# One score block in eighteen exponentiated on VectorE, with a new model of the convolution's load times

## The chip, the cores and the metric

The kernel runs on one core of one Trainium2 chip. The metric is the device time of one execution in microseconds (us). A time is the median of several executions. A profile is one execution, and its span is about 2 us shorter than the time. A core has five engines with a queue each: TensorE (PE in the profile, PEld its weight loads), VectorE (DVE), ScalarE (ACT), GpSimd (POOL) and SyncE (SP, which here issues loads). The program gives each engine one list of instructions, and before an instruction the engine waits until the semaphores that it names are reached.

## The reference

Two independent results stand side by side in the output: attention with 32 heads of 16, and a long causal convolution with gates.

```python
qkv = (x @ wqkv).reshape(B, S, 3, H, Dh).transpose(2, 0, 3, 1, 4)      # S 2048, D 512, H 32, Dh 16
scores = einsum("bhqd,bhkd->bhqk", q, k) * Dh ** -0.5
p = softmax(scores, axis=-1)
a = einsum("bhqk,bhkd->bhqd", p, v).transpose(...).reshape(B, S, D) @ wo
# ... k_shift: a 4-tap shift of B_k; kv = k_shift * B_v
y = causal_convolution(kv, ssm_k) + kv * ssm_D      # by FFT in the reference; 512 channels, 2048 taps each
b = B_q * y
out = concatenate([a, b], axis=-1)
```

The attention has 32 x 2048 x 2048 exponentials. The kernel makes them as 2048 blocks of 128 x 512.

## The kernel before

Scores lie in PSUM, three banks to a "chunk", two sets of three banks in turn. A step T of the main loop does one chunk: TensorE makes three score blocks (`emit_qk`), ScalarE exponentiates all three in one instruction of 1536 columns, TensorE multiplies earlier blocks by the values (`emit_pv`), and one piece of background work follows (`emit_bg`): convolution matmuls, projections, output products. There are 692 steps. A "group" (4 heads x 512 queries) is 64 blocks, some 21.3 steps. When it is done, `finish_group` normalises it with five VectorE instructions.

```python
    def emit_qk(T):
        # ... three matmuls of a chunk; wait for bank_free of the three banks
        h = pe.op(fn, deps)
        n = len(bl)
        h_exp[T] = act.op(lambda e: e.activation(PT[:, T % R_PT, 0:n * QB],
                                                 PS[:, banks[0]:banks[0] + n, :].rearrange("p b f -> p (b f)"),
                                                 ACT.Exp, scale=SCALE),
                          [h, h_ptfree.get(T - R_PT)])
        for bank in banks:
            bank_free[bank] = h_exp[T]
```

All background work shares one PSUM bank (`BGB`). VectorE copies each finished piece out of it ("evacuation"), and the next piece of background work waits for that copy. TensorE's next scores stand behind that piece in its list, so while it waits there it makes no scores either (one such place, with a wait of 2.26 us, is shown below).

```python
    def conv_lags(qd, n0, n1):
        # ... 4 matmuls per lag into bank BGB; after four rows-of-four:
                hh = dve.op(lambda e: e.tensor_copy(YB[:, half, :].rearrange("p (k i) -> p k i", k=4), src),
                            [h, h_yb[0]])
                bank_free[BGB] = hh
    # ...
    for T in range(NT + 3):
        if T < NT:
            emit_qk(T)
        # ...
        while pvs:
            emit_pv(pvs[:4], T)
            pvs = pvs[4:]
        emit_bg(T)
        for item in list(dve_later):      # the rest of a group's normalisation, one and two steps later
            if item[0] <= T:
                dve_later.remove(item)
                item[1]()
```

The convolution reads 512 filter matrices of 512 KB ("rows") from HBM, 12 in flight. When the program is built, a small model guesses when each four rows have landed, so that no convolution matmul is put in the queue too early:

```python
    def now(T):
        return 11.0 + 1.17 * min(T, N_EARLY) + 1.345 * max(T - N_EARLY, 0)
    # at the start: first rows expected 10.5, 16.5, 22.5 us after now(T); later 1.5 us a row
```

The softmax here doesn't subtract the row's maximum and nothing guards it: scores larger than these inputs give would overflow.

## Time and profile before

| | before |
|---|---|
| time, median of 3 runs | 989.31 us (989.12 to 989.63) |
| span of the profile | 986.4 us |
| ScalarE busy | 937.7 us (95%) |
| VectorE busy | 236.1 us (24%) |
| ScalarE idle between 150 and 950 us | 3.3 us (800 - 796.72) |

First come the busy times of the engines, their share of the span and their instructions, and the shares of the chain of waits, which is followed back from the last instruction.

```profile
PE 767.7 (78%) x12892; PEld 333.4 (34%) x12892; DVE 236.1 (24%) x386; ACT 937.7 (95%) x699; POOL 46.7 (5%) x65
...
ACT 79%; PE 11%; DVE 5%; DMA 4%; SPq 1%; issue 1%; ACTq 0%
```

Next, pieces of the same chain in order of time (start, duration, what; xN is the number of instructions merged).

```profile
119.06 21.19 DMA WR<-kz_scratch
...
144.98 134.69 ACT PT L459 x99
...
357.78 171.30 ACT PT L459 x126
```

134.69 / 99 and 171.30 / 126 both give 1.36 us for a back-to-back exponential of 1536 columns. These long runs without another engine between them mean that ScalarE is the limit. The DMA piece at 119 us is the one early place where everybody waits for the first convolution rows; ScalarE idles 7.3 us there.

The stretches view has the busy time of each engine in a window; the last three numbers are TensorE's granted clock, the DMA share and GB/s.

```profile
core 0: us, PE busy (x) PEld busy (x) DVE busy (x) ACT busy (x) POOL busy (x), PEclk, DMA share, GB/s
150.00:950.00 800.00, 611.31 (x11814) 284.26 (x11814) 139.80 (x217) 796.72 (x587) 13.61 (x18) 0.97 0.90 332
```

Two lines of the timeline show exponentials that stood alone, in the early part where TensorE is the limit (start, duration, engine, line, instruction, in brackets the idle time before and what ended it).

```profile
12.18 1.45 ACT L459 ACTIVATE PT<-PS 128x1536 bf16<-128x1536 f32 x1 [0.58 <-PE PS L452]
14.32 1.02 ACT L459 ACTIVATE PT<-PS 128x1024 bf16<-128x1024 f32 x1 [0.69 <-PE PS L452]
```

512 columns more cost 0.43 us more. That is what a block taken from ScalarE can save.

### The profile page before, as it was taken

How to read it: one execution, taken by the hardware profiler on the slowest of the kernel's cores; microseconds unless marked ns; L12 is line 12 of the kernel's file. 1: busy time of each engine (PE TensorE's matmuls, PEld its weight loads, DVE VectorE, ACT ScalarE, POOL GpSimd, SP SyncE). 2: the span in 40 equal slices, each digit the busy share in tenths (PEclk: the TensorE clock that was granted, in tenths of full speed). 3: DMA queues.
4: the chain of work that ended last, by engine and by line, in shares of the span. 5: the costliest groups of instructions: out<-in, count | busy, mean ns of one | idle time of the engine just before them, and what ended most of it. 6: DMA issues, size and time to landing. Idle time of an engine off the chain costs nothing.

```text
span 986.4 us, 27802 instructions
## 1 busy us (share of the span) xinstructions
PE 767.7 (78%) x12892; PEld 333.4 (34%) x12892; DVE 236.1 (24%) x386; ACT 937.7 (95%) x699; POOL 46.7 (5%) x65
## 2 busy tenths in 40 slices
PE   8998867878787787777777787777777787777787
PEld 3322123333333333333333333333333333333312
DVE  4778611211121210121211021212011212111111
ACT  5887869999999999999999999999999999999996
POOL 2121400000000100000001000000000000000000
PEclk9999779999999989999999999999999999999957
DMA  9441499998989999999899999998999999798300
GB/s 315 170 149 65 135 320 344 327 366 320 356 308 353 342 363 349 355 334 357 330 367 323 366 341 349 342 358 329 359 349 348 345 341 340 290 352 344 142 22 22
DMA packets 88566, 295.56 MB, mean 300 GB/s; under 512 B 11269, under 2 KB 19458, under 8 KB 88066
## 3 DMA queue, kind: packets, MB, share of 16 engines
q1 hardware_dynamic: 82114, 280.13, 76.8%
q0 software_dynamic: 3936, 12.58, 4.0%
q8 instruction: 102, 1.67, 0.7%
q10 hardware_dynamic: 2400, 1.05, 0.4%
q14 instruction: 14, 0.11, 0.0%
HBM read 287.31 MB, written 6.42 MB: 298 GB/s over the span
## 4 chain that ended last, share of the span: by engine, by line
ACT 79%; PE 11%; DVE 5%; DMA 4%; SPq 1%; issue 1%; ACTq 0%
ACT PT L459 78%; DMA WR<-kz_scratch 4%; PE PS L452 2%; PE PS L289 2%; PE PS L282 2%; PE PS L485 1%; PE PS L552 1%; PE PS L600 1%; DVE VAF L317 1%; SPq L151 1%; DVE WR L352 1%; DVE WR L356 1%; DVE KTo L311 1%; PE PS L275 1%; PE PS L393 1%
## 5 line engine op out<-in xcount | busy, mean ns | idle before, releaser
L459 ACT ACTIVATE PT<-PS 128x1536 bf16<-128x1536 f32 (+1 forms) x692 | 932.5, 1799 | 31.6 <-PE PS L452 31.5
L452 PE MATMUL PS<-QT,KTo 32*128 32x512 bf16 x2048 | 284.0, 404 | 188.1 <-ACT PT L459 181.5
L600 PE MATMUL PS<-WR,KV 128*15 128x128 bf16 (+15 forms) x8192 | 298.3, 226 | 16.7 <-DMA WR<-kz_scratch 11.1
L485 PE MATMUL PS<-PT,VAF 128*32 128x512 bf16 x2048 | 289.6, 409 | 0.9 <-DVE VAF L317 0.5
L600 PEld LDWEIGHTS PS<-WR,KV 128*13 128x13 bf16 (+15 forms) x8192 | 191.4, 107 | 40.7 <-issue 27.4
L452 PEld LDWEIGHTS PS<-QT,KTo 32*128 32x128 bf16 x2048 | 67.9, 92 | 367.1 <-ACT PT L459 332.5
L485 PEld LDWEIGHTS PS<-PT,VAF 128*32 128x32 bf16 x2048 | 69.2, 94 | 170.3 <-issue 162.5
L616 DVE CAST YB<-PS 128x512 bf16<-128x512 f32 x32 | 22.1, 691 | 372.5 <-PE PS L600 313.7
L505 DVE COPY OF<-PS 128x512 f32<-128x512 f32 x31 | 21.6, 696 | 217.6 <-PE PS L485 193.9
L275 PE MATMUL PS<-xT,WQP 128*128 128x512 bf16 x128 | 38.9, 397 | 1.2 <-ACT xT L261 0.3
L552 PE MATMUL PS<-WKV,OTN 128*128 128x512 bf16 x128 | 35.9, 398 | 1.3 <-DVE YB L616 1.1
L303 DVE CAST QT<-PS 128x512 bf16<-128x512 f32 x32 | 22.0, 689 | 50.6 <-PE PS L275 50.6
L151 POOL DMA_DIRECT2D out_dram<-OUTA x12 | 6.6, 551 | 405.3 <-DVE OUTA L560 378.9
L514 DVE STREAM_TRANSPOSE DT<-DR 128x512 f32<-128x512 f32 x32 | 23.1, 721 | 1.1
L507 DVE STREAM_TRANSPOSE DT<-OF 128x512 f32<-128x512 f32 x31 | 22.8, 734 | 1.1
L151 POOL DMA_DIRECT2D out_dram<-QN x4 | 4.7, 1172 | 379.3 <-DVE QN L636 379.3
L520 DVE TENSOR_TENSOR OTN<-OF,DT 128x512 bf16<-128x512 f32 x31 | 22.1, 714 | 0.8
L282 PE MATMUL PS<-xT,WKV 128*128 128x512 bf16 x64 | 18.3, 413 | 3.2 <-DVE KTo L311 1.1
L289 PE MATMUL PS<-WKV,xT 128*128 128x512 bf16 x64 | 16.6, 382 | 1.5 <-DVE xT L263 0.2
L352 DVE TENSOR_TENSOR WR<-WR 128x1024 bf16<-128x1024 bf16 x24 | 16.3, 683 | 0.0
L552 PEld LDWEIGHTS PS<-WKV,OTN 128*128 128x128 bf16 x128 | 9.8, 101 | 18.8 <-issue 9.5
L151 POOL DMA_DIRECT2D WR<-in_B_k_dram x20 | 13.9, 701 | 40.3 <-DVE KV L361 30.3
(53 smaller groups left out, 175.5 us busy)
## 6 DMA issues: line engine op xcount, KB each, us to landing
WR<-kz_scratch SPq DMA_DIRECT2D x512, 512.0 KB, 7.6
WR<-in_B_k_dram POOLq DMA_DIRECT2D x16, 256.0 KB, 4.9
kz_scratch<-WR SPq DMA_DIRECT2D x1, 2176.0 KB, 8.9
KV<-in_A_x_dram SPq DMA_DIRECT2D x4, 512.0 KB, 6.6
QN<-in_B_q_dram POOLq DMA_DIRECT2D x4, 512.0 KB, 11.3
out_dram<-QN POOLq DMA_DIRECT2D x4, 512.0 KB, 7.9
WR<-in_B_v_dram SPq DMA_DIRECT2D x6, 256.0 KB, 3.2
QT<-in_B_k_dram POOLq DMA_DIRECT2D x6, 256.0 KB, 4.3
```

The lines of the kernel that those rows point to most:

```text
L151: f(outp, inp).then_inc(dsem.sem, 16)
L275: return e.matmul(PS[:, bank, :], lhsT=WQP[:, dc, g, :], rhs=xT[:, dc, qb * 512:(qb + 1) * 512], start=(dc == 0), stop=(dc == 3))
L282: return e.matmul(PS[:, bank, :], lhsT=WK[:, dc, o * 128:(o + 1) * 128], rhs=xT[:, dc, sc * 512:(sc + 1) * 512], start=(dc == 0), stop=(dc ...
L289: return e.matmul(PS[:, bank, :], lhsT=xT[:, dc, kt * 128:(kt + 1) * 128], rhs=WV[:, dc, :], start=(dc == 0), stop=(dc == 3))
L352: st[m] = dve.op(lambda e: e.tensor_tensor(b[m], b[m], in1, ALU.mult), [h_kv[(j, 0)], h_kv[(j, 1)], h_tb[m]])
L452: ins = e.matmul(PS[:, bank, :], lhsT=KTo[32 * s:32 * s + 32, g // 2, kt * 128:(kt + 1) * 128], rhs=QT[32 * s:32 * s + 32, qb % 2, g, :], ...
L459: h_exp[T] = act.op(lambda e: e.activation(PT[:, T % R_PT, 0:n * QB], PS[:, banks[0]:banks[0] + n, :].rearrange("p b f -> p (b f)"), ACT.E ...
L485: ins = e.matmul(PS[32 * s:32 * s + 32, pvb(qb * NG + g), :], lhsT=VAF[:, kt, h * VW:h * VW + 32], rhs=PT[:, Tc % R_PT, j * QB:(j + 1) * Q ...
L507: h_t = dve.op(lambda e: e.transpose(out=DT[:, r, :], in_=src), [h_of, h_otn.get(n - 2)])
L514: st["h"] = dve.op(lambda e: e.transpose(out=DT[:, r, :].rearrange("p (b i) -> p b i", i=32), in_=rcp.broadcast_to([128, 16, 32])), [h])
L552: ins = e.matmul(PS[:, bank, :], lhsT=OTN[:, oslot(qb * NG + g), t * 128:(t + 1) * 128], rhs=WOP[:, g, :], start=(g == 0), stop=(g == NG - 1))
L600: ins = e.matmul(PS[32 * c:32 * c + NB - n, BGB, 128 * (kk % 4):128 * (kk % 4) + 128], lhsT=KV[:, n:NB, d], rhs=WR[:, d % R_W, 128 * (NB - ...
```

## The change

VectorE is idle three quarters of the time, and ScalarE is the limit. So the last block of some chunks is exponentiated on VectorE. By the rule of the change 113 chunks from step 86 on are touched, one block in each, at most four to a group (chunks 2, 7, 12 and 17 of it); that is one in 18 of the 2048 blocks; ScalarE's instruction in such a chunk has 1024 columns. VectorE scales the scores so that the integer part of the exponential's base-2 logarithm falls into the exponent field of a floating-point number, splits exponent and fraction by bit operations, and evaluates a quartic in the fraction. That gives the exponential times a constant 2 / C4. So that all blocks of a row agree, ScalarE's exponentials get the same factor: a bias of ln(2 / C4), read from a tile `EB` of one number per partition. Softmax divides the factor out again.

The model of load times is changed too: the first rows are expected later, a row is taken to need 1.3 instead of 1.5 us, and the steps are timed anew.

```diff
+    h_eb = dve.op(lambda e: e.memset(EB[:], math.log(2.0 / C4)))
+    on_dve = {}
+    for T in range(N_EARLY + 30, NT):
+        # ... n: the group, t0: its first chunk
+        if len(bl) == 3 and n == blk_group(bl[0]) and (T - t0) % 5 == 2 and T <= chunk_of[last_blk[n]][0] - 3 and 0 < kt < KT - 1:
+            on_dve[bl[-1]] = len(on_dve)
@@ emit_qk
-        n = len(bl)
+        n = len(bl) - (bl[-1] in on_dve)
-                                                 ACT.Exp, scale=SCALE),
+                                                 ACT.Exp, bias=EB[:, 0:1], scale=SCALE),
+        if n < len(bl):
+            bank_free[banks[n]] = exp_on_dve(bl[n], banks[n], h, T)
+    def exp_on_dve(b, bank, h, T):
+        h1 = dve.op(lambda e: e.tensor_scalar(EI[:, :], PS[:, bank, :], FIX, FIX_LO, ALU.mult, ALU.max), [h, h_eo[0]])
+        # split(): EM = (EI & 0x7fffff) | 0x3f800000; EI = (EI & 0x7f800000) ^ 0x40000000
+        # horner(j): EH = (src + B) * m, three times;  last(): PTD = (EH + B0) * EI as fp32, to bf16
+        dve_fill.extend([(T, split), (T + 1, lambda: horner(0)), (T + 1, lambda: horner(1)),
+                         (T + 2, lambda: horner(2)), (T + 2, last)])
+        return h1
@@ now, emit_bg
-        return 11.0 + 1.17 * min(T, N_EARLY) + 1.345 * max(T - N_EARLY, 0)
+        t1 = N_EARLY + 30
+        return 12.0 + 1.36 * min(T, t1) + 1.266 * max(T - t1, 0)
-            st["dma"] = now(T) + 3.0
+            st["dma"] = now(T) + 18.0
             for i in range(R_W // 4):
-                st["dma"] += 6.0
-                    st["dma"] = max(st["dma"], now(T) + 3.0) + 1.5
+                    st["dma"] = max(st["dma"], now(T) + 3.0) + 1.3
@@ the values' matmul of a moved block comes 5 steps after its chunk instead of 2
-        t = chunk_of[b][0] + 2
+        t = chunk_of[b][0] + (5 if b in on_dve else 2)
@@ main loop
+        for item in list(dve_fill):
+            if item[0] <= T:
+                dve_fill.remove(item)
+                item[1]()
         emit_bg(T)
```

More of the change, by code (lines that the diff above doesn't have):

```diff
@@ L1 @@
+import math
 import concourse.bass as bass
@@ L7 @@
 FP32 = mybir.dt.float32
+INT32 = mybir.dt.int32
 S = 2048
@@ L33 @@
 LAGS = 5
+C4 = 0.013534167911703966
+B0, B1, B2, B3 = 37.6797618003151, 23.053950042922654, 12.310574509367148, -0.15702561410827162
+LOG2E = 1.4426950408889634
+FIX = SCALE * LOG2E * 2.0 ** 23
+FIX_LO = -126.0 * 2.0 ** 23
 class Eng:
@@ L124, in bass_concat_heads__mha_block__ssm_conv_h3__prompt_kernel @@
     SHK = sb("SHK", [128, 4, 4])
+    PTD = sb("PTD", [128, 2, QB])
+    EI = sb("EI", [128, QB], INT32)
+    EM = sb("EM", [128, QB], INT32)
+    EH = sb("EH", [128, QB], FP32)
+    EB = sb("EB", [128, 1], FP32)
     JNK = sb("JNK", [128, 2], FP32)
@@ L432, in pvb @@
         return BGB if n == 1 else PVB
-    h_exp = {}
-    h_ptfree = {}
     chunk_of = {}
@@ L439, in bass_concat_heads__mha_block__ssm_conv_h3__prompt_kernel, with blk_group @@
             chunk_of[b] = (T, j)
+    def blk_group(i):
+        qb, g, kt, s = blk(i)
+        return qb * NG + g
+    on_dve = {}
+    for T in range(N_EARLY + 30, NT):
+        bl = chunks[T][0]
+        qb, g, kt, s = blk(bl[-1])
+        n = qb * NG + g
+        t0 = chunk_of[first[n]][0]
+        if len(bl) == 3 and n == blk_group(bl[0]) and (T - t0) % 5 == 2 and T <= chunk_of[last_blk[n]][0] - 3 and 0 < kt < KT - 1:
+            on_dve[bl[-1]] = len(on_dve)
+    h_exp = {}
+    h_blk = {}
+    h_ptfree = {}
     def emit_qk(T):
@@ L457, in emit_qk, with split, horner, last @@
         h = pe.op(fn, deps)
-        n = len(bl)
+        n = len(bl) - (bl[-1] in on_dve)
         h_exp[T] = act.op(lambda e: e.activation(PT[:, T % R_PT, 0:n * QB],
                                                  PS[:, banks[0]:banks[0] + n, :].rearrange("p b f -> p (b f)"),
-                                                 ACT.Exp, scale=SCALE),
-                          [h, h_ptfree.get(T - R_PT)])
-        for bank in banks:
-            bank_free[bank] = h_exp[T]
+                                                 ACT.Exp, bias=EB[:, 0:1], scale=SCALE),
+                          [h, h_ptfree.get(T - R_PT), h_eb])
+        for b, bank in zip(bl[:n], banks):
+            bank_free[bank] = h_blk[b] = h_exp[T]
+        if n < len(bl):
+            bank_free[banks[n]] = exp_on_dve(bl[n], banks[n], h, T)
+    h_eo = [None]
+    h_ptd = {}
+    def exp_on_dve(b, bank, h, T):
+        i = on_dve[b]
+        m = EM[:, :].bitcast(FP32)
+        st = {}
+        h1 = dve.op(lambda e: e.tensor_scalar(EI[:, :], PS[:, bank, :], FIX, FIX_LO, ALU.mult, ALU.max), [h, h_eo[0]])
+        def split():
+            st["m"] = dve.op(lambda e: e.tensor_scalar(EM[:, :], EI[:, :], 0x7fffff, 0x3f800000,
+                                                       ALU.bitwise_and, ALU.bitwise_or), [h1])
+            st["e"] = dve.op(lambda e: e.tensor_scalar(EI[:, :], EI[:, :], 0x7f800000, 0x40000000,
+                                                       ALU.bitwise_and, ALU.bitwise_xor), [st["m"]])
+        def horner(j):
+            src = m if j == 0 else EH[:, :]
+            st["h"] = dve.op(lambda e: e.scalar_tensor_tensor(EH[:, :], src, (B3, B2, B1)[j], m, ALU.add, ALU.mult),
+                             [st["m"], st.get("h")])
+        def last():
+            h_blk[b] = h_eo[0] = dve.op(
+                lambda e: e.scalar_tensor_tensor(PTD[:, i % 2, :], EH[:, :], B0, EI[:, :].bitcast(FP32),
+                                                 ALU.add, ALU.mult), [st["h"], st["e"], h_ptd.get(i - 2)])
+        dve_fill.extend([(T, split), (T + 1, lambda: horner(0)), (T + 1, lambda: horner(1)),
+                         (T + 2, lambda: horner(2)), (T + 2, last)])
+        return h1
+    dve_fill = []
     def oslot(n):
@@ L472, in emit_pv @@
     def emit_pv(bl, T):
-        deps = [h_exp[chunk_of[b][0]] for b in bl] + [h_v[blk(b)[2]] for b in bl]
+        deps = [h_blk[b] for b in bl] + [h_v[blk(b)[2]] for b in bl]
         for b in bl:
@@ L484, in fn @@
                 Tc, j = chunk_of[b]
+                rhs = PTD[:, on_dve[b] % 2, :] if b in on_dve else PT[:, Tc % R_PT, j * QB:(j + 1) * QB]
                 ins = e.matmul(PS[32 * s:32 * s + 32, pvb(qb * NG + g), :],
                                lhsT=VAF[:, kt, h * VW:h * VW + 32],
-                               rhs=PT[:, Tc % R_PT, j * QB:(j + 1) * QB],
+                               rhs=rhs,
                                start=(kt == 0), stop=(kt == KT - 1), tile_position=(0, 32 * s))
@@ L491, in emit_pv @@
         for b in bl:
-            h_ptfree[chunk_of[b][0]] = h
+            if b in on_dve:
+                h_ptd[on_dve[b]] = h
+            else:
+                h_ptfree[chunk_of[b][0]] = h
         for b in bl:
@@ L765, in bass_concat_heads__mha_block__ssm_conv_h3__prompt_kernel @@
     assert state["qd"] == C // 4 and not state["turn"] and state["q"] == len(later_q) and state["op"] == len(later_op), state
-    assert not dve_later and not kv_pieces
+    assert not dve_later and not kv_pieces and not dve_fill
     qb = NQB - 1
```

## The prediction

> **What bounds it now.** ScalarE. The stretches view has it busy 796.7 of the 800 us between 150 and 950; the chain of waits gives 78% of the span to the exponentials. Long runs of that chain (99 in 134.69 us, 126 in 171.30 us) give 1.36 us per 1536-wide exponential, of which 0.08 us is fixed if a column costs 0.833 ns. Until about 142 us (86 of 692 steps) TensorE and VectorE bound it; there one wait for the convolution's loads idles ScalarE 7.3 us. VectorE is busy 24%. DMA moves about 350 GB/s but reaches 410 to 416 in 6-us stretches: not at its limit.
>
> **What changes.**
> 1. By the diff's rule 113 of the last 606 steps (4 per group) give ScalarE 1024 columns instead of 1536. Isolated exponentials took 1.45 and 1.02 us: 113 x 0.43 = 48 us less ScalarE work, all on the critical path.
> 2. VectorE gets seven instructions per moved block: one from PSUM (0.69 us, as its other 512-wide PSUM reads), two integer ones in SBUF (0.42 us each, an estimate from the two-port mode for single-source fp32 in the Trainium skill, "VectorE: DVE Perf Modes", perf-mode tier table; no trace here shows it), four two-operand fp32 (0.71 us by the 512-wide fp32 multiply). About 4.5 us a block, 510 us: VectorE goes to some 75%, about 85% in the steady part. Evacuations wait behind it, by up to a step where a group finishes. TensorE idles about 0.36 us per step and scores are made nearly a step ahead, so I expect only 5 us lost.
> 3. The later first convolution piece removes most of the 7.3 us wait. The load model (1.3 us a row, 403 GB/s) is within what the trace shows; 0 to 5 us of new waits.
> 4. All 692 exponentials now read their bias from a [128,1] tile in SBUF; before it was a constant. The Trainium skill, "ScalarE: Activation LUTs", What ACT_TABLE_LOAD costs: an ACTIVATE with constants takes 186 ns + 0.833 ns per column (1.47 us for 1536; the trace has 1.45 isolated), "each [128,1] pointer operand adds ≈ 93 ns". If that also lengthens the step in back-to-back runs, it costs 606 x 0.093 = 56 us, plus some 3 earlier, all critical. No run here shows this yet. The next pointer might be fetched during the current instruction, but the 0.08 us left in every back-to-back step suggests that operands are not fetched ahead.
>
> **Sum.** With the bias cost in full: 989 - 48 + 59 - 7 + 5 = about 998, less what the early part hides: about 990 us; a plain step becomes 1.45, a short one 1.02, the mean 1.37. With it hidden: about 940. With half: 960. I hold the first likeliest (0.55 to 0.6). Predicted 988 us, range 936 to 1006; faster by over 2%: 0.37, within 2%: 0.54, slower: 0.09.
>
> **What would show it.** 1536-wide exponentials isolated at 1.54 instead of 1.45, back to back at 1.45 instead of 1.36, ScalarE busy near 940 us: the bias costs. Unchanged durations, busy near 890: hidden. VectorE busy near 745 us, the integer pair at 0.42 us (0.69 means no fast mode). The wait for the first loads gone from the chain. ScalarE idle in the steady part below 2%.
>
> **What would make it wrong.** The hidden bias (then 5% faster). VectorE in the way: a late first read of a moved block holds a score bank, and evacuations hold the bank of the background work; if ScalarE idles over 3%, the time passes 1006. Convolution matmuls waiting for loads because the model runs ahead.

## The result, and the profile after

| | before | after |
|---|---|---|
| time, median of 4 runs | 989.47 us (989.12 to 990.24) | 1027.3 us (1024.91 to 1029.83) |
| span of the profile | 986.4 us | 1023.1 us |
| ScalarE busy | 937.7 us | 955.3 us |
| ScalarE idle over the span | 48.7 us | 67.8 us |
| ScalarE idle, 0 to 150 us | 35.9 us | 23.0 us |
| ScalarE idle, 150 to 950 us | 3.3 us | 34.4 us |
| VectorE busy | 236.1 us | 702.6 us |

The ratio is 1.038 (95% interval 1.035 to 1.041): 3.8% slower. In the profiles the span grew by 36.7 us: 17.6 us of ScalarE work and 19.1 us of ScalarE idle time.

The engines' busy times and the chain's shares after the change, and in the second block the stretches view from 150 to 950 us:

```profile
PE 809.2 (79%) x12892; PEld 350.5 (34%) x12892; DVE 702.6 (69%) x1178; ACT 955.3 (93%) x699; POOL 46.7 (5%) x65
...
ACT 65%; PE 17%; DVE 16%; issue 1%; DMA 1%; ACTq 0%
```

```profile
150.00:950.00 800.00, 617.75 (x11590) 294.27 (x11590) 561.36 (x934) 765.64 (x557) 12.43 (x17) 0.95 0.89 332
```

ScalarE's share of the chain fell from 79 to 65%, and TensorE and VectorE took it: the chain now leaves ScalarE again and again.

Isolated exponentials in the timeline, and a piece of the chain in order of time with ten plain ones in a row, before any block is moved:

```profile
12.36 1.54 ACT L490 ACTIVATE PT<-PS,EB 128x1536 bf16<-128x1536 f32 x1 [0.58 <-PE PS L483]
14.51 1.11 ACT L490 ACTIVATE PT<-PS,EB 128x1024 bf16<-128x1024 f32 x1 [0.60 <-PE PS L483]
```

```profile
105.68 14.44 ACT PT L490 x10
```

An isolated exponential takes 0.09 us more (1.54 for 1.45, 1.11 for 1.02), and a back-to-back one 1.444 instead of 1.36. The mean over the window is 765.64 / 557 = 1.375 us. Before it was 796.72 / 587 = 1.357 us, so the moved blocks did not even pay for the bias tile.

The VectorE instructions of a moved block, by group (busy total, mean duration in ns, idle before):

```profile
L506 DVE TENSOR_SCALAR EI<-PS 128x512 int32<-128x512 f32 x113 | 79.4, 702 | 182.8 <-PE PS L483 182.5
L509 DVE TENSOR_SCALAR EM<-EI 128x512 int32<-128x512 int32 x113 | 47.8, 423 | 3.2
L511 DVE TENSOR_SCALAR EI<-EI 128x512 int32<-128x512 int32 x113 | 49.7, 440 | 3.9
L516 DVE SCALAR_TENSOR_TENSOR EH<-EM 128x512 f32<-128x512 f32 x113 | 78.6, 695 | 0.0
L516 DVE SCALAR_TENSOR_TENSOR EH<-EH,EM 128x512 f32<-128x512 f32 x226 | 159.8, 707 | 6.4
L521 DVE SCALAR_TENSOR_TENSOR PTD<-EH,EI 128x512 bf16<-128x512 f32 x113 | 79.3, 701 | 3.9
```

The busy totals add to 494.6 us, 4.4 us a block. Where the new idle time comes from is seen in one place of the timeline, where a group finishes (VectorE, then TensorE, then ScalarE):

```profile
618.44 0.69 DVE L506 TENSOR_SCALAR EI<-PS 128x512 int32<-128x512 f32 x1 [3.90 <-PE PS L483]
619.05 0.68 DVE L572 COPY OF<-PS 128x512 f32<-128x512 f32 x1
...
623.43 0.65 DVE L516 SCALAR_TENSOR_TENSOR EH<-EH,EM 128x512 f32<-128x512 f32 x1
624.11 0.69 DVE L521 SCALAR_TENSOR_TENSOR PTD<-EH,EI 128x512 bf16<-128x512 f32 x1
624.72 0.68 DVE L587 TENSOR_TENSOR OTN<-OF,DT 128x512 bf16<-128x512 f32 x1
625.33 0.68 DVE L683 CAST YB<-PS 128x512 bf16<-128x512 f32 x1
...
622.32 0.44 PE L667 MATMUL PS<-WR,KV 128*1 128x128 bf16 x4
...
626.07 0.82 PE L619 MATMUL PS<-WKV,OTN 128*128 128x512 bf16 x3 [2.26 <-DVE YB L683]
...
627.26 1.11 ACT L490 ACTIVATE PT<-PS,EB 128x1024 bf16<-128x1024 f32 x1 [1.36 <-PE PS L483]
```

The convolution's last matmuls of this piece (L667) start at 622.32 us, so the bank can be emptied soon after. But VectorE is in the middle of an unbroken run that began at 618.44: the first read of a moved block, the normalisation of the group, the polynomial. The evacuation (L683) starts at 625.33. TensorE stands 2.26 us at the next background product (L619), the scores come late, and ScalarE idles 1.36 us. A place in before where a group has just finished looks like this:

```profile
605.68 0.44 PE L600 MATMUL PS<-WR,KV 128*1 128x128 bf16 x4
606.18 0.69 DVE L616 CAST YB<-PS 128x512 bf16<-128x512 f32 x1 [3.54 <-PE PS L600]
607.35 0.82 PE L552 MATMUL PS<-WKV,OTN 128*128 128x512 bf16 x3
```

The cast starts 0.5 us after those last matmuls, where in after it starts 3.0 us after them, and TensorE does not wait for it. Between 150 and 950 us of before the longest wait of a matmul for this cast was 0.9 us.

This place is no exception. I added up, from the timelines of ScalarE and VectorE between 150 and 850 us, the idle time of ScalarE that ended less than 12 us after the start of a group's normalisation (the copy to `OF`). In after that is 26.0 of 34.8 us (this count comes out some 2 us above the table's idle time), in before 1.5 of 3.2. A group takes some 29 us (21.3 steps of 1.375).

### The profile page after: what moved, and what is told of

Its sections match the earlier page's. It is cut to its first block, busy times and chain, and to the rows that moved or that the text cites. A ratio compares the mean times of both kernels' runs of the same rounds, so it can differ in the third digit from the quotient of the medians. Undisturbed runs are those within 1.5% of the kernel's fastest.

```text
span 1023.1 us, 28781 instructions
## 1 busy us (share of the span) xinstructions
PE 809.2 (79%) x12892; PEld 350.5 (34%) x12892; DVE 702.6 (69%) x1178; ACT 955.3 (93%) x699; POOL 46.7 (5%) x65
## 4 chain that ended last, share of the span: by engine, by line
ACT 65%; PE 17%; DVE 16%; issue 1%; DMA 1%; ACTq 0%
ACT PT L490 64%; PE PS L483 5%; DVE EH L516 3%; PE PS L549 3%; PE PS L667 3%; PE PS L619 2%; DVE EI L506 2%; PE PS L306 2%; PE PS L292 1%; PE PS L299 1%; DVE DT L574 1%; DVE OF L572 1%; DVE EM L509 1%; DVE YB L683 1%; DVE EI L511 1%
## 5 line engine op out<-in xcount | busy, mean ns | idle before, releaser
L490 ACT ACTIVATE PT<-PS,EB 128x1536 bf16<-128x1536 f32 (+1 forms) x692 | 950.1, 1531 | 49.6 <-PE PS L483 47.5
L667 PE MATMUL PS<-WR,KV 128*16 128x128 bf16 (+15 forms) x8192 | 312.6, 230 | 19.0 <-DVE QT L320 8.4
L667 PEld LDWEIGHTS PS<-WR,KV 128*14 128x14 bf16 (+15 forms) x8192 | 206.3, 106 | 51.7 <-issue 34.3
L506 DVE TENSOR_SCALAR EI<-PS 128x512 int32<-128x512 f32 x113 | 79.4, 702 | 182.8 <-PE PS L483 182.5
L516 DVE SCALAR_TENSOR_TENSOR EH<-EH,EM 128x512 f32<-128x512 f32 x226 | 159.8, 707 | 6.4
L521 DVE SCALAR_TENSOR_TENSOR PTD<-EH,EI 128x512 bf16<-128x512 f32 x113 | 79.3, 701 | 3.9
L516 DVE SCALAR_TENSOR_TENSOR EH<-EM 128x512 f32<-128x512 f32 x113 | 78.6, 695 | 0.0
L511 DVE TENSOR_SCALAR EI<-EI 128x512 int32<-128x512 int32 x113 | 49.7, 440 | 3.9
L509 DVE TENSOR_SCALAR EM<-EI 128x512 int32<-128x512 int32 x113 | 47.8, 423 | 3.2
L619 PE MATMUL PS<-WKV,OTN 128*128 128x512 bf16 x128 | 39.7, 432 | 11.1 <-DVE YB L683 7.5
L549 PE MATMUL PS<-PTD,VAF 128*32 128x512 bf16 x113 | 48.3, 427 | 0.2 <-DVE PTD L521 0.2
L320 DVE CAST QT<-PS 128x512 bf16<-128x512 f32 x32 | 22.0, 687 | 27.6 <-PE PS L292 27.6
L683 DVE CAST YB<-PS 128x512 bf16<-128x512 f32 x32 | 21.9, 685 | 8.9 <-PE PS L667 8.5
```

The lines of the kernel that those rows point to most:

```text
L506: h1 = dve.op(lambda e: e.tensor_scalar(EI[:, :], PS[:, bank, :], FIX, FIX_LO, ALU.mult, ALU.max), [h, h_eo[0]])
L509: st["m"] = dve.op(lambda e: e.tensor_scalar(EM[:, :], EI[:, :], 0x7fffff, 0x3f800000, ALU.bitwise_and, ALU.bitwise_or), [h1])
L511: st["e"] = dve.op(lambda e: e.tensor_scalar(EI[:, :], EI[:, :], 0x7f800000, 0x40000000, ALU.bitwise_and, ALU.bitwise_xor), [st["m"]])
L516: st["h"] = dve.op(lambda e: e.scalar_tensor_tensor(EH[:, :], src, (B3, B2, B1)[j], m, ALU.add, ALU.mult), [st["m"], st.get("h")])
L521: lambda e: e.scalar_tensor_tensor(PTD[:, i % 2, :], EH[:, :], B0, EI[:, :].bitcast(FP32), ALU.add, ALU.mult), [st["h"], st["e"], h_ptd.ge ...
L549: ins = e.matmul(PS[32 * s:32 * s + 32, pvb(qb * NG + g), :], lhsT=VAF[:, kt, h * VW:h * VW + 32], rhs=rhs, start=(kt == 0), stop=(kt == K ...
```

## The experiments

**Theory A.** Two costs: the bias tile lengthens every exponential also in back-to-back runs, and evacuations stand behind moved blocks in VectorE's queue. **Rivals.** B: the bias read is hidden. C: moved blocks cost by holding their score bank until VectorE's late first read. D: the new load model sends convolution matmuls ahead of their loads. All runs had three timed rounds beside the kernel before; e1 to e4 ran on one chip, e5 to e8 on a second, e9 to e11 on a third. The medians of before in the three sets were 990.38, 990.0 and 989.24 us.

| run | change | median us (4 runs) | ratio to before | ScalarE idle, 150 to 850 us |
|---|---|---|---|---|
| before | | 989.47 | | 3.3 |
| after | | 1027.3 | 1.038 | 32.9 |
| e1 | after, constant bias | 995.47 | 1.005 | 56.9 |
| e2 | before, bias tile | 1042.49 | 1.053 | 4.9 |
| e3 | after, other places | 1001.38 | 1.011 | 15.5 |
| e4 | before, load model | 983.0 | 0.993 | 3.7 |
| e5 | constant bias, places | 967.91 | 0.979 | 27.6 |
| e6 | constant bias, places, order | 946.53 | 0.955 | 11.3 |
| e7 | VectorE's load without benefit | 1021.37 | 1.033 | 34.2 |
| e8 | benefit without polynomial (wrong) | 945.02 | 0.956 | 12.6 |
| e9 | constant bias, order | 973.87 | 0.985 | 32.7 |
| e10 | after, order | 1008.04 | 1.017 | 24.2 |
| e11 | e6 with a fifth block | 977.87 | 0.988 | 41.2 |

The idle column is 700 us less ScalarE's busy time in that window of the profile. A profile is one execution: those of e1, e2, e3 and e10 are of the slowest of their four, e1's 6 us above its median, and that of after is of its fastest.

### e1: the bias as a constant

```diff
-  ACT.Exp, bias=EB[:, 0:1], scale=SCALE),
+  ACT.Exp, bias=math.log(2.0 / C4), scale=SCALE),
```

> The changed kernel with one thing undone: the exponentials take their bias as a constant again instead of from the [128,1] tile; everything else stays. Theory A (the bias read costs about 0.085 us per back-to-back exponential and the rest of the loss is ScalarE idle behind a crowded VectorE queue): plain steps return from 1.44 to 1.36 us back to back, isolated 1536-wide ones from 1.54 to 1.45, ScalarE busy falls by 50 to 60 us from 955 to about 898, but VectorE has less time per block, so ScalarE idle grows; time 975 to 995. Rival B (the bias read is hidden and the changed kernel is slow for VectorE and load reasons alone): time stays within 1% of the changed kernel, 1017 to 1037.

Measured: 995.47 us (992.44 to 1001.76), just over the top of the stated range, and 32 us less than after. Isolated exponentials are back at 1.45 us. ScalarE's busy time fell by 56.1 us to 899.2, as expected. But its idle time between 150 and 850 us rose from 32.9 to 56.9 us, as the theory has it for a ScalarE that leaves VectorE's queue less time; part of that rise may be the slow execution that was profiled. Its stretches view from 150 to 850 us:

```profile
150.00:850.00 700.00, 550.92 (x10257) 260.51 (x10279) 500.50 (x831) 643.15 (x495) 12.44 (x17) 0.94 0.91 339
```

B falls.

### e2: the kernel before with a bias tile

```diff
-  ACT.Exp, scale=SCALE),
+  ACT.Exp, bias=EB[:, 0:1], scale=SCALE),      # EB: [128,1], zeros; awaited once
```

> The kernel before with one thing added: every exponential reads a zero bias from a [128,1] tile; no block is moved, the load model is the old one. Theory A: +0.085 us on each of the about 630 exponentials that run back to back, all on the critical path: 989 + 50 to 56 = 1039 to 1047 us, plain steps 1.44 us, ScalarE idle unchanged. Rival B: 989 plus at most 5.

Measured: 1042.49 us (1038.24 to 1046.41), in the range. ScalarE idle between 150 and 950 us is 8.9 us, little more than before. Two pieces of its chain:

```profile
142.79 96.83 ACT PT L461 x67
...
583.18 157.56 ACT PT L461 x109
```

96.83 / 67 and 157.56 / 109 give 1.445 us, 0.086 us more than before, on an otherwise unchanged kernel. This run also answers another question: its mean granted TensorE clock is the lowest of these profiles (0.904; before 0.946, after 0.923), and still ScalarE hardly idles. So a lower clock alone does not make this idle time; that it adds to it in after, where some steps are shorter, is not excluded.

### e3: the moved blocks away from the normalisation

```diff
-  (T - t0) % 5 == 2 and T <= ...
+  (T - t0) % 4 == 1 and T - t0 >= 5 and T <= ...
```

> The changed kernel with the moved blocks at other places: chunks 5, 9, 13 and 17 of a group instead of 2, 7, 12 and 17, so that none shares its steps with the normalisation of the group before (chunks 2 to 4); 114 blocks instead of 113. The bias tile stays. Theory A (VectorE's queue is crowded where a group finishes, evacuations that TensorE needs stand behind it): the waits of background matmuls for VectorE's evacuations fall from the some 50 us to under half, ScalarE's idle time between 150 and 950 us from 34 us to under 18, time 1004 to 1015. Rival C (each moved block costs by itself, by holding its score bank until VectorE's late first read): idle stays at 30 us or more, time 1022 to 1032.

Measured: 1001.38 us (996.83 to 1004.72), 26 us less than after with one block more, and just under the stated range. ScalarE idle between 150 and 950 us halved, from 34.4 to 17.1 us; in the 12 us after the start of a normalisation it fell from 26.0 to 2.9 us. C, which said that it stays, falls. One part of my expectation missed: the total of the waits of TensorE's matmuls for VectorE between 150 and 850 us fell only from 44.3 to 35.2 us. Here are the three largest waits for the convolution's cast between 150 and 950 us in after (who, for whom: total us, times, longest), and below them the same in e3.

```profile
PE PS L292 <- DVE YB L683: 8.9, 7, 2.9
PE PS L694 <- DVE YB L683: 7.7, 8, 2.5
PE PS L619 <- DVE YB L683: 7.5, 4, 2.8
```

```profile
PE PS L694 <- DVE YB L683: 6.7, 8, 1.1
PE PS L292 <- DVE YB L683: 4.5, 5, 1.1
PE PS L619 <- DVE YB L683: 1.9, 3, 0.8
```

Their sum fell from 24.1 to 13.1 us, and the longest wait from 2.9 to 1.1 us. In before TensorE waits for ScalarE some 0.3 us in each step (174.5 us in 587 steps between 150 and 950 us), so short waits can be absorbed; in the place shown above, 0.9 us of the 2.26 were. Both the sum and the longest wait count. At nearly equal sums of TensorE's waits for VectorE (150 to 850 us) and with the same bias, the run with the shorter longest wait idles less: e3 (sum 35.2, longest 1.1) idles 15.5 us, e10 (33.2 and 2.4) 24.2; e5 (35.8 and 1.4) 27.6, e9 (37.1 and 2.7) 32.7. But with the constant bias even waits of at most 1.4 us leave 27.6 us of idle time (e5).

### e4: the load model alone

```diff
 # in the kernel before: now(), first rows at now + 18, 1.3 us a row, as in the change
```

> The kernel before with the new model of the load times alone: first pieces later, 1.3 us a row, the new clock of steps. No moved block, no bias tile. Theory A: the 7.3 us wait of ScalarE for the first loads goes, nothing else changes: 980 to 984 us. Rival D (the faster model sends the convolution ahead of its loads, and that is part of the loss): 990 to 1010, with waits of convolution matmuls for loads of over 10 us.

Measured: 983.0 us (980.02 to 983.49), ratio 0.993 (0.990 to 0.995): the model alone is a gain of 7 us. Between 105 and 152 us ScalarE's wait for scores fell from 8.7 to 3.1 us, so part of the early wait remains. Convolution matmuls wait 3.9 us for loads between 150 and 950 us, and in after itself 1.5 us between 150 and 850. D falls.

### e5: constant bias and other places

The edits of e1 and e3 together.

> The changed kernel with both: bias as a constant and the moved blocks at chunks 5, 9, 13 and 17 of a group. If the two costs are separate and add, the constant takes some 30 us and the places some 25 to 35 us off 1027: 955 to 970 us, faster than the kernel before by 2 to 3.5%; ScalarE idle between 150 and 950 us 25 to 40 us, against 60 with the old places. If the places do not matter once ScalarE is faster (VectorE is simply too full), it stays near 990.

Measured: 967.91 us (966.84 to 974.57), idle 27.6 us between 150 and 850 us, as expected.

### e6: and evacuations first

```diff
+        emit_bg(T)
         for item in list(dve_fill):
             if item[0] <= T:
                 dve_fill.remove(item)
                 item[1]()
-        emit_bg(T)
```

> As e5, and in each step the evacuation of the background work is put into VectorE's queue before that step's polynomial instructions instead of behind them. If evacuations standing behind polynomial instructions are what is left, 5 to 15 us less than e5, and TensorE's waits for evacuations fall by half. Rival: VectorE, which runs in order, now stands idle at evacuations that TensorE has not produced yet, and the time rises by 5 us or more.

Measured: 946.53 us (941.23 to 949.96), ratio 0.955 (0.950 to 0.961): 4.5% faster than the kernel before, and correct. The gain over e5 is 21 us, more than I had expected. TensorE's waits for VectorE between 150 and 850 us fell from 35.8 to 13.4 us. Busy times, and the stretches view from 150 to 850 us:

```profile
PE 788.9 (83%) x12892; PEld 345.4 (37%) x12892; DVE 724.0 (77%) x1185; ACT 894.5 (95%) x699; POOL 46.9 (5%) x65
```

```profile
150.00:850.00 700.00, 577.62 (x11135) 278.50 (x11132) 555.72 (x900) 688.67 (x534) 12.50 (x17) 0.98 0.97 366
```

VectorE does the work of after (724 us, with one block more), and ScalarE is busy 95% again.

### e7: VectorE's load without the benefit

```diff
 # on e1: ScalarE exponentiates all three blocks, TensorE uses them; VectorE's first instruction is
-  e.tensor_scalar(EI[:, :], PS[:, bank, :], FIX, FIX_LO, ALU.mult, ALU.max)
+  e.scalar_tensor_tensor(EI[:, :], EH[:, :], FIX, EH[:, :], ALU.mult, ALU.max)
 # bank_free of every score bank is ScalarE's again; the values' matmul is 2 steps after, as before
```

> VectorE's load alone, without its benefit: the constant bias, ScalarE exponentiates all three blocks of every chunk again, TensorE uses its result, and VectorE runs the same seven instructions at the old places on a tile of its own in SBUF, so that it holds no score bank; its results go nowhere. The result is right. Theory A (the queue in front of the evacuations is the loss): against 983 us of the load model alone (the fourth run) 25 to 45 us more, 1008 to 1028, ScalarE idle between 150 and 950 us 25 to 40 us. Rival C (the held score bank is the loss): within 5 us of 983.

Measured: 1021.37 us (1018.95 to 1030.09), 38 us over e4 (1.033 of before against 0.993), with 34.2 us of ScalarE idle against 3.7 (and 942.8 us of ScalarE busy time against 937.0). No bank is held here and no moved block is waited for. Below are the stretches views of e4 and of e7, in which ScalarE has the same exponentials to make (ScalarE's busy time, then granted clock, DMA share and GB/s):

```profile
150.00:850.00 700.00, 696.27 (x513) 0.96 0.94 351
150.00:850.00 700.00, 665.79 (x486) 0.94 0.89 333
```

The queue by itself costs as much idle time as after has (32.9 us), and at the same place: by the count above 24.3 of 35.7 us lie in the 12 us after the start of a normalisation. This is the cleanest evidence against C. (A variant in which both engines read the same bank without waiting for each other was refused by the check before it could be submitted. The held bank was therefore not tried by itself.)

### e8: the benefit without the polynomial

```diff
 # on e1, wrong on purpose
-  e.tensor_scalar(EI[:, :], PS[:, bank, :], FIX, FIX_LO, ALU.mult, ALU.max)  + six more
+  e.tensor_scalar(PTD[:, i % 2, :], PS[:, bank, :], SCALE, 1.0, ALU.mult, ALU.add)
```

> The benefit alone, wrong on purpose: the constant bias, ScalarE spared the 113 blocks, VectorE makes only the first read of each moved block, straight to bf16 (a straight line instead of an exponential, and without the common factor), and no polynomial. It holds the score bank as before. Theory A: 989 - 7 - 48 + 0 to 8 for the rest = 934 to 945 us, ScalarE idle between 150 and 950 us under 12 us. Rival C (the held bank): ScalarE idle stays above 30 us, time 960 or more.

Measured: 945.02 us (943.46 to 950.71), at the top of the stated range, with a wrong result (relative error 0.203). Idle between 150 and 850 us is 12.6 us, slightly over the 12 expected for the longer window. With the bank still held until VectorE's first read, but the polynomial gone, the loss is gone. e6, with the polynomial, is as fast as this. So in e6 the polynomial's load on VectorE costs nothing more that these two runs, whose places and order differ too, can tell apart.

### e9 and e10: the order alone

e9 is e1 with the order of e6; e10 is after with the order of e6 (places and bias tile stay).

> The changed kernel with the constant bias and the evacuations ahead of the same step's polynomial instructions, the moved blocks at their old places (chunks 2, 7, 12, 17). Against e1 (995) it shows the order alone, against e6 (946) the places alone. If the order is the main part: 955 to 965 us, ScalarE idle between 150 and 850 us 18 to 28 us (e1: 57, e6: 11). If order and places are about equal in worth and add: 965 to 978.

> The changed kernel with nothing but the order changed: evacuations ahead of the same step's polynomial instructions; bias tile and old places stay. Theory A: 1027 less 15 to 25, 1000 to 1012 us, with ScalarE idle between 150 and 850 us from 33 to under 18 us. Rival: the gain appears only with the constant bias, because a slower ScalarE leaves the queue time: 1020 or more.

Measured: e9 973.87 us (970.17 to 977.11), 22 us under e1; e10 1008.04 us (999.1 to 1010.86), 19 us under after. e9 lies in the branch in which order and places are about equal in worth and add. The order helps with either bias. In e10 I expected ScalarE idle under 18 us and measured 24.2: the places still matter.

### e11: a fifth block

```diff
-  (T - t0) % 4 == 1 and T - t0 >= 5 and T <= ...
+  (T - t0) % 4 == 1 and T <= ...
```

> As e6 with one more moved block per group, at chunk 1 (some 142 instead of 114). If ScalarE is still what bounds it: 28 x 0.43 = 12 us less, 932 to 938. If the loads (366 GB/s and 97% busy in e6) or VectorE (77% busy) now bound it: 943 to 960, with more of TensorE's waits for loads or for evacuations.

Measured: 977.87 us (974.0 to 980.29), 31 us over e6, worse than both branches of my expectation. 132 blocks are moved, 18 more. The window shows it:

```profile
150.00:850.00 700.00, 557.75 (x10665) 268.97 (x10697) 596.39 (x978) 658.78 (x515) 12.47 (x17) 0.96 0.94 352
```

ScalarE idles 41.2 us, against 11.3 in e6, and the waits for VectorE are back at 49.3 us. Not the loads: matmuls wait 6.7 us for them, against 9.0 in e6. The new block stands at chunk 1, just before a normalisation, and VectorE is also fuller (82% busy). The trace tells part of the two: of ScalarE's idle time, counted as above, 26.4 us lie in the 12 us after the start of a normalisation, against 5.4 in e6, and 15.7 us elsewhere, also against 5.4. So about two thirds of the new idle time stand where the new block was put, and a third elsewhere.

## Why the prediction was wrong

Point by point, with the prediction's own numbers:

- **ScalarE bounds it: right.** Every gain and loss above is ScalarE's work or its idle time.
- **The bias tile costs in full: right.** Predicted 0.093 us per exponential, isolated 1.54, plain 1.45, mean 1.37. Measured 0.086 in back-to-back runs (e2), 1.54, 1.444 and 1.375. The change from e1 to after is 56 us of ScalarE work. The prediction's "near 940" for ScalarE's busy time did not even follow from its own sum (937.7 - 48 + 59 = 949); measured were 955.3. The moved blocks saved less than 48 us of busy time: 37.8 us between e4 and e1, but 46.6 between e4 and e8, which hardly idles. That fits the 0.09 us by which an exponential behind a gap is longer than a back-to-back one (1.45 and 1.36), but was not tested by itself.
- **VectorE's work per block: right.** 0.42 us for the integer pair (0.423 and 0.440), 0.70 for the rest, 4.4 us a block. VectorE's total is 703 us where I said near 745.
- **The load model: right.** e4 shows 7 us of gain and no new wait worth the name.
- **"So I expect only 5 us lost": the step that failed.** This is the term for evacuations waiting behind VectorE. Measured: ScalarE idle between 150 and 950 us rose from 3.3 to 34.4 us, 31 us in place of 5. e7 shows 38 us from the queue alone, without any of the benefit, and e3 and e10 show that places and order alone take 26 and 19 us back. The mechanism was named, and so was its threshold (over 3% idle, time over 1006); the size was wrong. I reckoned with the mean slack of a step. The idle time comes in bursts instead: where a moved block and the normalisation of a group fall together, about 7 us of instructions stand in front of one evacuation, and TensorE stands for 2.3 us; three quarters of ScalarE's idle time in after (26.0 of 34.8 us) end within 12 us of the start of a normalisation.

The parts are nearly additive. From 1027.3 us the constant bias takes 32, the places 26, the order 19, together 77; all three at once (e6) take 81. What stays open: how much a held score bank costs by itself in after, and how much of the third of e11's new idle time that lies elsewhere is VectorE being fuller.

## What to carry to other kernels

Before moving work to an idle engine, list what else stands in that engine's queue and who waits for it: the average load says little (e6 idles ScalarE 11.3 us with VectorE 77% busy, after 32.9 us with 69%), the runs of instructions in front of a short, urgent one say more. Put the urgent instruction first and place the new work away from existing bursts; here that and one operand form turned 3.8% slower into 4.5% faster with the same arithmetic and one moved block more. And check what a change does to instructions that it seems only to touch in passing: a per-partition bias on every exponential cost more than the moved blocks saved.

## What the Trainium skill lacked or had wrong

- "ScalarE: Activation LUTs", What ACT_TABLE_LOAD costs: the page gives 93 ns per pointer operand and 93 ns of overlap, but does not say outright whether the cost remains in back-to-back runs. It does: 0.086 us (1.360 to 1.445, e2), and 0.09 isolated (1.45 to 1.54).
- The same page, Rules for kernel authors, calls ScalarE "the only option" for `exp`. VectorE made 114 blocks of 128 x 512 in seven instructions and about 4.4 us each, with a correct result, in a kernel 4.5% faster (e6).
- "VectorE: DVE Perf Modes", the perf-mode tier table: the table names neither integer types nor `scalar_tensor_tensor` (other pages of the skill treat what the modes need, but give no time for these two). The runs show 0.42 to 0.44 us for a 128 x 512 int32 `tensor_scalar` in SBUF, in line with the 2x mode that the table gives `tensor_scalar` on fp32 in SBUF, and 0.70 us for the fp32 `scalar_tensor_tensor`.
- "Perfetto Trace Analysis", Optimizing Scalar/DVE Operations, advises to break up instructions where an unsaturated VectorE causes bubbles elsewhere. It says nothing of the order in the queue, which alone was worth 19 us here on a VectorE 70% busy (e10), and no instruction had to be broken up.
